# One-core attention and bilinear FFN kernel: kept outputs stored one stage sooner, loads two units ahead, weight sums one at a time, two half masks through ACT and GpSimd

## The chip, the cores and the metric

The kernel runs on one core of a Trainium2 chip. The metric is the device time of one execution in microseconds, and the value compared is the median over runs. The kernel before takes 241.34 us (median of 3 runs, 240.53 to 241.75).

## The reference

The work is a linear attention with decay, followed by a bilinear feed-forward layer. Cut to what matters (B = 4 batches, H = 8 heads, S = 768 positions, D = 64; d_model = 512, d_ff = 1536):

```
for each block of positions:                      # reference: 64, kernel: 128
    intra = ((q_b k_b^T) * decay_mask) v_b        # lower triangle only
    inter = (q_b * lam^(pos+1)) kv_state
    out_b = intra + inter
    kv_state = lam^block * kv_state + (k_b * lam^(block-1-pos))^T v_b
x = out, as [3072 tokens, 512]
y = ((x @ w_a) * (x @ w_b)) @ w_out
```

## The kernel before

**Units and groups.** A unit is 128 positions of one batch with all its heads; there are 24, numbered 0 to 23. They go through the feed-forward layer (FFN) in eight groups (`GROUPS`, L28): group 0 has units 0 to 3, group 1 unit 4, group 2 units 5 and 6, groups 3 to 6 four units each (7 to 10, 11 to 14, 15 to 18, 19 to 22), group 7 unit 23. While PE multiplies the FFN of one group, the attention of the next group's units is slipped in between its products.

**Attention of a unit.** `qf`, `kf` and `vf` are loaded by DMAs on SP's queue (L136). GpSimd (POOL in the profile) scales `kf` and `qf` into the bf16 tile `qk` (L282), and `vb` is the bf16 copy of `vf` (L299 on ACT, L301 on POOL or DVE, chosen in `make_vb`). From unit 7 on, `qk` is transposed by a DMA, also on SP's queue (L312). PE makes the scores `kq` in two PSUM banks, one for even and one for odd heads (L340). DVE multiplies each bank with the triangle `lotri` into the masks `m0` and `m1` (L357). PE then makes `o_ps` from the state (`inter`) and from the masks (`intra`, L374), and ACT copies it into `xT` (L397). The state is accumulated in `kvd` and copied to `st` by DVE (L437).

**FFN of groups 0, 1, 2 and 7** (`ffn`): for each of 12 columns f of 128, `a_ps` and `b_ps` are made (L477), ACT copies a (`a_sb`, L486), DVE multiplies it with b into `ab` (L504). Then, for each unit, 12 products with `wo_sb` give `op` (L647).

**FFN of groups 3 to 6** (`ffn_seven`): the two weights, the two halves of the contraction and the two halves of the 512 tokens form 2 x 2 blocks, which are multiplied with seven products in place of eight, for each of six column pairs i. For that, sums of the weights (`tw`, four operations of DVE for each i, L512 to L515 in `w_sums`) and sums of `xT` (`xs`, L524 to L527) are needed. In each i, PE writes `m_q`, `m_r` and `m_p` (L544), ACT copies them out (L559), POOL adds `c11` (L579) and multiplies `ab` (L588), DVE does the rest (L586, L592, L595).

**What sets the order.** Every engine runs its own instructions in the order in which the program writes them, and so does SP's queue of DMAs. FFN code calls `hook(slot)` at fixed places, and the table `PLAN` says which step is written there: `PK` scales q and k and issues the transposing DMA (`prep_k`), `PV` casts v (`prep_v`) and calls `pump`, `P` does both, `S` is scores and masks, `Q` and `O2` are the attention of two units (with `Q` the scores of two more), `V` the state, `TW` the sums of the weights, `W` one store of a kept output. Slots 0 to 11 lie between the FFN's products, slot 12 and up between the `op` products. In groups 3 to 5 the steps `PK` of two units of the following groups are at slots 11 and 12, and `P` of two more at slots 16 and 18.

**Loads.** `pump` (L194) issues the next loads in order, for as many units beyond `used["u"]` as the line with `LOOKAHEAD` allows (L200): 3, but 2 while `used["u"]` lies between 9 and 16, and 1 at 10. q and k have three buffers each, v has four.

**Stores.** The outputs of groups 0 to 2 (7 units) stay in tiles `o_kept`, and seven steps `W` store them (L631). Later outputs go through `o_sb`, a pool with three buffers: ACT copies `op` into it (L642) and SP stores it (L643). The fourth copy of a group needs the buffer of the first.

**Banks and buffers.** Seven PSUM banks are taken in turn. The pool `wst` has 13 buffers for staged weights, `tw`, `xs`, `o_kept` and the tile `s12` of each i; the pool `a` has five, for `a_sb` and `c11`.

Of the kernel before, what the change touches and what calls it, by code (L numbers as in the profile page):

```python
# [17 lines left out]
BF16 = mybir.dt.bfloat16  # L18
# [4 lines left out]
def _bc(ap, dims):  # L23
# [9 lines left out]
LOOKAHEAD = {9: 2, 10: 1}  # L33
# [10 lines left out]
PLAN = {  # L44
# [18 lines left out]
    else:  # L63
        PLAN[_g] += [(14, "PV", _u + 5), (16, "P", _u + 6), (18, "P", _u + 7), (19, "S", _u + 5)]
PLAN[3] += [(1, "PK", 13), (3, "PK", 14), (8, "PV", 13), (11, "PV", 14)]
PLAN[3] += [(_s, "W", None) for _s in range(12, 19)]
PLAN[0] += [(7, "TW", (0, "dve")), (7, "TW", (1, "dve")), ]
PLAN[1] += [(8, "TW", (4, "dve")), (11, "TW", (5, "dve"))]


@with_exitstack
def kernel(
# [15 lines left out]
    HP = H // 2  # L88
# [9 lines left out]
    wst_pool = ctx.enter_context(tc.tile_pool(name="wst", bufs=W_BUFS + 2))  # L98
# [5 lines left out]
    a_pool = ctx.enter_context(tc.tile_pool(name="a", bufs=5))  # L104
# [28 lines left out]
    def load_x(w, u):  # L133
        b, nb = divmod(u, NB)
        t = ld_pool.tile([128, H, D], F32, name=w + "f", tag=w + "f", bufs=4 if w == "v" else 3)
        nc.sync.dma_start(out=t, in_={"q": qr, "k": kr, "v": vr}[w][b, nb])  # L136
        raw[u, w] = t
# [16 lines left out]
    def load_w(kind, c):  # L154
        t = wst_pool.tile([128, 1024], F32, name="wst", tag="wst")
        if kind == "o":
            t = t[:].rearrange("p (k n) -> p k n", k=2)
            nc.sync.dma_start(out=t, in_=wo_r[:, 2 * c:2 * c + 2, :])
        else:
            w = W_CHUNKS[c]  # L160
            t = t[:, :KS * w].rearrange("p (k n) -> p k n", k=KS)
            r = wa_r if kind == "a" else wb_r
            if c in W_HALVES:
                t = t.rearrange("p k n -> p (k n)").rearrange("p (k n) -> p k n", k=2)
            nc.sync.dma_start(out=t, in_=w_part(r, c))
        staged[kind, c] = t
# [20 lines left out]
    n0 = GROUPS[0]  # L187
# [4 lines left out]
    used = {"u": 0}  # L192

    def pump():  # L194
        while pending:
            kind, c = pending[0]
            if kind in "abo":
                if len(staged) >= W_BUFS:
                    return
            elif c >= used["u"] + LOOKAHEAD.get(used["u"], 2 if 8 < used["u"] < 17 else 3):  # L200
                return
            pending.pop(0)
            if kind in "abo":
                load_w(kind, c)
            else:
                load_x(kind, c)
# [15 lines left out]
    for w, src in (("q", q), ("k", k)):  # L222
# [3 lines left out]
        for c in range(0, HP, n_c):  # L226
            t = wst_pool.tile([128, 1024], F32, name=w + "4", tag="wst")[:, :n_c * 512]
            t = t.rearrange("p (c b x) -> p c b x", c=n_c, b=2)
# [4 lines left out]
    for u in range(n0):  # L233
        load_x("v", u)
    pump()


# [40 lines left out]
    def eng_of(name):  # L278
        return nc.gpsimd if name == "pool" else nc.vector
# [15 lines left out]
    def make_vb(u, eng):  # L295
        vb = prep_pool.tile([128, H, D], BF16, name="vb", tag="vb", bufs=5)
        vf = raw.pop((u, "v"))
        if eng == "act":
            nc.scalar.copy(vb, vf)  # L299
        else:  # L300
            eng_of(eng).tensor_copy(vb, vf)  # L301
        U[u]["vb"] = vb
# [12 lines left out]
            U[u]["qT"], U[u]["kT"] = qkT[:, 0], qkT[:, 1]  # L315

    def prep_v(u):
        make_vb(u, "pool" if u < n0 + 3 else "dve" if u < n0 + 7 else "act")
        pump()

    def piece_T(u):
# [20 lines left out]
        return kq  # L342

    def masks(u, kq):
        ms = mask(kq)
        U[u]["m"] = lambda i, hp: ms[i][:, hp, :]

    def mask(kq, split=False):
        ms = []
        for i in range(2):  # L350
            m = msk_pool.tile([128, HP, 128], BF16, name=f"m{i}", tag=f"m{i}")
            if split and i == 1:
                raw_kq = scr[0][:, 8:9, :].rearrange("p s (h j) -> p (s h) j", h=HP)
                nc.scalar.copy(raw_kq, kq[i])
                nc.gpsimd.tensor_mul(m, raw_kq, lotri_bc)
            else:
                nc.vector.tensor_mul(m, kq[i], lotri_bc)  # L357
            ms.append(m)
        return ms
# [80 lines left out]
    def piece_S(u):  # L440
        masks(u, scores(u))
# [8 lines left out]
    def pieces_O(us, nxt=()):  # L450
        kqs = [score_banks() for u in nxt]
        o_banks(us)
        for u, kq in zip(nxt, kqs):
            scores(u, kq)
        for u in us:
            inter(u)
        for b in range(2):
            for u in us:
                intra(u, b)
            evac_o(us, b)  # L460
        sums(us[-1])
        beside = len(us) == 2 and us[0] >= n0 + 5
        if beside:
            kv_beside(us[1])
        for u, kq in zip(nxt, kqs):
            masks(u, kq)
        if beside and us[1] % NB < NB - 1:
            kv_copy(us[1], kv["ps"])
# [34 lines left out]
        ps = half(wb_sb, f, xT, "b_ps", 0, gt)  # L503
        nc.vector.tensor_mul(ab[:, f, :gt], a_sb[:, :gt], ps[:, :gt])  # L504

    def w_sums(i, eng):
        t = wst_pool.tile([128, 4, 2, 256], BF16, name="tw", tag="wst")
        tw[i] = t
        e = nc.gpsimd if eng == "pool" else nc.vector
        c = slice(256 * i, 256 * i + 256)  # L510
        a1, a2, b1, b2 = wa_sb[:, 0:2, c], wa_sb[:, 2:4, c], wb_sb[:, 0:2, c], wb_sb[:, 2:4, c]
        e.tensor_sub(t[:, 0], b1, a1)  # L512
        e.tensor_sub(t[:, 1], b2, t[:, 0])
        e.tensor_sub(t[:, 2], b2, b1)
        e.tensor_sub(t[:, 3], a2, t[:, 1])  # L515

    def sums(u):
        g = next(i for i in range(len(GROUPS)) if g_u0[i] <= u < g_u0[i] + GROUPS[i])
# [11 lines left out]
    tw, xs = {}, {}  # L530
# [180 lines left out]
    scr = [ab_pool.tile([128, FC, 512], BF16, name="scratch", tag="ab") for _ in range(2)]  # L711
# [44 lines left out]
    def scores4(i, ups, ats):  # L756
        kqs = []
        for up, at in zip(ups, ats):
            kq = [ps_bank(f"kq{par}", [128, HP, 128], F32, at=at[par]) for par in range(2)]
            for uu in range(2):  # L760
                cols = slice((2 * up + uu) * BLK, (2 * up + uu + 1) * BLK)
                for j in range(2):
                    for par in range(2):
                        p = slice(64 * par, 64 * par + 64)
                        nc.tensor.matmul(kq[par][:, 2 * uu + j, :],
                                         lhsT=xT4["k"][p, 2 * i + j, cols],
                                         rhs=xT4["q"][p, 2 * i + j, cols],
                                         start=True, stop=True, skip_group_check=True)
            kqs.append(kq)
        for up, kq in zip(ups, kqs):  # L770
            ms4[i, up] = mask(kq, split=(i == 1 and up == 1))
# [65 lines left out]
    for g, n in enumerate(GROUPS):  # L837
# [6 lines left out]
        def hook(slot, plan=plan):  # L844
            for name, us in plan.get(slot, ()):
                if name == "C":
                    cast_w("o", us, "dve")
                elif name == "PK":
                    prep_k(us)
                elif name == "PV":  # L850
                    prep_v(us)
                elif name == "P":
                    prep_k(us)
                    prep_v(us)
                elif name == "TW":
                    w_sums(*us)
                elif name == "W":
                    store_kept()
                elif name == "T":
                    piece_T(us)  # L860
                elif name == "S":
                    piece_S(us)
                elif name == "V":
                    piece_V(us)
                elif name == "O":
                    pieces_O((us,))
                elif name == "O2":
                    pieces_O(us)
                else:
                    pieces_O(us[:2], us[2:])  # L870
# [34 lines left out]
```

## Time and profile before

| | |
|---|---|
| median of 3 runs | 241.34 us (240.53 to 241.75) |
| the profiled execution's own time | 242.57 us |
| its span | 240.8 us |
| mean granted TensorE clock | 0.972 |
| PE busy | 221.3 us (92%) |
| DVE, ACT, POOL busy | 143.9, 118.8, 108.2 us |
| DMA | 39.40 MB, mean 164 GB/s |

Times in the rows of the timeline are microseconds from the span's start: the first number is the start, the second how long the row lasts, then engine, line, operation, out<-in. x is the number of instructions merged in a row; a bracket gives the idle time before it and what ended that. A row of SPq is the issue of a DMA on SP's queue: it lasts until the queue goes on to the next, not until the data has landed. The rows of DMA issues give the time from the start of the issue to the landing. In the list of waits, a row gives the total, the number of waits and the longest. The groups of the profile come in this order in the span: group 1 from about 51.5 to 66.5, group 2 to 88, group 3 to 122, group 4 to 163, group 5 to 202.

### The profile page before, as it was taken

The numbers are of one execution on the slowest core, as the hardware profiler recorded it, in microseconds if no ns is written. First come the engines' busy times: TensorE is split into PE (matmuls) and PEld (weight loads), VectorE is DVE, ScalarE is ACT, GpSimd is POOL, SyncE is SP. The second block draws the span as 40 slices with busy tenths as digits, with TensorE's granted clock in tenths as the row PEclk, the third lists the DMA queues.
The fourth block names the chain that finished last, engine by engine and source line by source line (L and its number), as shares of the span: only waits on it lengthen the run. The fifth ranks groups of instructions, "written<-read, shape, count | busy, mean of one in ns | idle before, by whom it ended". The sixth has DMA issues, their size and how long they took to land.

```text
span 240.8 us, 5405 instructions
## 1 busy us (share of the span) xinstructions
PE 221.3 (92%) x2127; PEld 151.1 (63%) x2127; DVE 143.9 (60%) x256; ACT 118.8 (49%) x233; POOL 108.2 (45%) x113
## 2 busy tenths in 40 slices
PE   7899999998799899999935999994999999999995
PEld 2465444477388468875514887543888557885494
DVE  1985788967967935688171567544566726664040
ACT  3686571165143277754414774543666236663151
POOL 6061001355530609997332778821677403874000
PEclk9999999999799999999995999998899999999999
DMA  4999999999999999903999990599100321000221
GB/s 147 303 270 354 369 386 314 243 207 203 203 166 178 193 209 216 184 18 70 235 227 289 278 217 0 78 206 295 36 0 0 91 87 46 0 4 0 91 86 44
DMA packets 97545, 39.40 MB, mean 164 GB/s; under 512 B 85489, under 2 KB 92017, under 8 KB 97521
## 3 DMA queue, kind: packets, MB, share of 16 engines
q1 hardware_dynamic: 97232, 39.00, 71.8%
q8 instruction: 16, 0.26, 0.5%
q10 hardware_dynamic: 288, 0.07, 0.1%
q14 instruction: 9, 0.07, 0.1%
HBM read 28.32 MB, written 6.29 MB: 144 GB/s over the span
## 4 chain that ended last, share of the span: by engine, by line
PE 64%; DMA 13%; POOL 8%; SPq 4%; DVE 4%; issue 3%; ACT 2%; POOLq 0%; ACTq 0%; DVEq 0%
PE op L647 18%; PE m_q L544 15%; PE a_ps L477 8%; PE b_ps L477 8%; PE m_r L544 7%; DMA vf<-in_v_dram 6%; POOL qk L282 4%; PE m_p L544 4%; SPq L136 3%; DMA out_dram<-o_sb 3%; DMA wst<-in_moe_w_a_dram 3%; POOL c L579 2%; DMA q<-in_q_dram 2%; PE o_ps L374 2%; POOL ab L588 1%
## 5 line engine op out<-in xcount | busy, mean ns | idle before, releaser
L647 PE MATMUL op<-wo_sb,ab 128*128 128x512 bf16 (+2 forms) x312 | 68.5, 368 | 3.9 <-DVE ab L504 2.7
L647 PEld LDWEIGHTS <-ab 128*128 128x128 bf16 x312 | 28.3, 98 | 32.0 <-issue 5.1
L579 POOL TENSOR_TENSOR c<-s 128x512 bf16<-128x512 f32 x24 | 30.6, 1273 | 37.0 <-ACT s L559 37.0
L544 PEld LDWEIGHTS <-tw 128*128 128x128 bf16 x384 | 38.2, 99 | 6.5
L504 DVE TENSOR_TENSOR ab<-a_sb,b_ps 128x128 bf16<-128x128 bf16 (+2 forms) x48 | 19.5, 418 | 22.9 <-ACT a_sb L486 16.2
L282 POOL TENSOR_TENSOR qk<-kf,lp_k 128x512 bf16<-128x512 f32 x18 | 19.1, 1059 | 30.6 <-DMA kf<-in_k_dram 14.1
L282 POOL TENSOR_TENSOR qk<-qf,lp_q 128x512 bf16<-128x512 f32 x20 | 21.9, 1093 | 22.0 <-DMA qf<-in_q_dram 22.0
L588 POOL TENSOR_TENSOR ab<-c,c 128x512 bf16<-128x512 bf16 x24 | 28.0, 1165 | 6.5 <-DVE c L586 6.1
L642 ACT COPY o_sb<-op 128x512 f32<-128x512 f32 (+2 forms) x19 | 10.3, 541 | 41.8 <-PE op L647 30.7
L357 DVE TENSOR_TENSOR m<-kq,lotri 128x512 bf16<-128x512 f32 x47 | 29.2, 681 | 2.0 <-PE kq L340 1.9
L595 DVE TENSOR_TENSOR ab<-c,m_q 128x512 bf16<-128x512 f32 x24 | 16.5, 688 | 22.8 <-PE m_q L544 22.8
L544 PE MATMUL m_q<-xs,tw 128*128 128x256 bf16 x192 | 29.9, 280 | 0.0
L477 PE MATMUL a_ps<-xT,wa_sb 128*128 128x128 bf16 (+2 forms) x200 | 27.7, 268 | 0.5 <-DVE wa_sb L177 0.5
L544 PEld LDWEIGHTS <-wa_sb 128*128 128x128 bf16 x192 | 19.3, 101 | 13.4 <-issue 10.0
L477 PE MATMUL b_ps<-xT,wb_sb 128*128 128x128 bf16 (+2 forms) x192 | 27.6, 272 | 0.0
L586 DVE TENSOR_TENSOR c<-u,m_r 128x512 f32<-128x512 f32 x24 | 16.4, 682 | 15.5 <-PE m_r L544 11.4
L544 PE MATMUL m_p<-xT,wa_sb 128*128 128x256 bf16 x96 | 15.2, 283 | 9.7 <-ACT o_sb L642 9.7
L486 ACT CAST a_sb<-a_ps 128x128 bf16<-128x128 f32 (+2 forms) x48 | 17.2, 376 | 13.7 <-PE a_ps L477 12.2
L477 PEld LDWEIGHTS <-wa_sb 128*128 128x128 bf16 x200 | 16.1, 98 | 7.2 <-DVE wa_sb L177 0.6
L559 ACT COPY s<-m_q 128x512 f32<-128x512 f32 x24 | 14.1, 587 | 13.0 <-PE m_q L544 12.0
L477 PEld LDWEIGHTS <-wb_sb 128*128 128x128 bf16 x192 | 15.8, 98 | 6.0 <-ACT wb_sb L175 0.2
L592 DVE TENSOR_TENSOR c<-s,m_q 128x512 f32<-128x512 f32 x24 | 16.5, 687 | 1.5 <-PE m_q L544 1.1
(85 smaller groups left out, 290.0 us busy)
## 6 DMA issues: line engine op xcount, KB each, us to landing
vf<-in_v_dram SPq DMA_DIRECT2D x24, 256.0 KB, 5.0
qf<-in_q_dram SPq DMA_DIRECT2D x20, 256.0 KB, 4.9
kf<-in_k_dram SPq DMA_DIRECT2D x20, 256.0 KB, 5.1
out_dram<-o_sb SPq DMA_DIRECT2D x16, 256.0 KB, 2.9
wst<-in_moe_w_a_dram SPq DMA_DIRECT2D x6, 512.0 KB, 8.5
wst<-in_moe_w_b_dram SPq DMA_DIRECT2D x6, 512.0 KB, 8.9
wst<-in_moe_w_out_dram SPq DMA_DIRECT2D x6, 512.0 KB, 10.6
out_dram<-o_kept SPq DMA_DIRECT2D x7, 256.0 KB, 3.9
```

Source lines behind the costliest of these rows:

```text
L282: eng_of(eng).tensor_mul(dst.rearrange("p (c b) d -> p b c d", b=2), x[:].rearrange("p (b c) d -> p b c d", b=2), lp.rearrange("p (b c) o ...
L357: nc.vector.tensor_mul(m, kq[i], lotri_bc)
L477: nc.tensor.matmul(ps[:, lo:hi], lhsT=w_sb[:, s, f * 128:(f + 1) * 128], rhs=xT[:, s, lo:hi], start=(s == 0), stop=(s == KS - 1), skip_gro ...
L486: nc.scalar.copy(a_sb[:, :gt], ps[:, :gt])
L504: nc.vector.tensor_mul(ab[:, f, :gt], a_sb[:, :gt], ps[:, :gt])
L544: nc.tensor.matmul(ps[:, f, :], lhsT=w(k, f), rhs=x[:, k, :], start=(first and f == 0 and k == 0), stop=True, skip_group_check=True)
L579: nc.gpsimd.tensor_add(d["c11"], d["s12"][:, 0], d["s12"][:, 1])
L586: nc.vector.tensor_add(c12, d["u2"], d["r"])
L588: nc.gpsimd.tensor_mul(ab[:, 2 * i:2 * i + 2, 0:256], d["c11"], c12)
L592: nc.vector.tensor_add(d["c22"], d["s5"], d["q"])
L595: nc.vector.tensor_mul(ab[:, 2 * i:2 * i + 2, 256:512], d["c22"], d["q"])
L647: nc.tensor.matmul(op[:, lo:hi], lhsT=ab[:, f, t * 128:(t + 1) * 128], rhs=wo_sb[:, f, lo:hi], start=(f == 0), stop=(f == FC - 1))
```

## The change

- The seven steps `W` move from slots 12 to 18 of group 3 to its slots 9 and 10.
- `pump` looks two units ahead for every `used["u"]` above 8; before, it was three from 17 on.
- The sums `tw` of i = 4 and i = 5 move from slots 8 and 11 of group 1, four operations in a row, to single operations in group 2: at slots 2, 3, 5, 6 (i = 4), and 8, 15, 15, 15 (i = 5).
- `vb` of units 9 and 10 is cast by ACT and no longer by DVE.
- Of units 7 and 8, the mask of the odd heads is made by a copy on ACT out of PSUM and a multiplication on GpSimd. The raw scores go to a buffer of the pool `a`; the split mask of group 0 now uses that too.

```diff
-PLAN[3] += [(_s, "W", None) for _s in range(12, 19)]
+PLAN[3] += [(_s, "W", None) for _s in (9, 9, 9, 10, 10, 10, 10)]
...
-PLAN[1] += [(8, "TW", (4, "dve")), (11, "TW", (5, "dve"))]
+PLAN[2] += [(_s, "TW", (4 + _n // 4, "dve", (_n % 4,)))
+            for _n, _s in enumerate((2, 3, 5, 6, 8, 15, 15, 15))]
...
-            elif c >= used["u"] + LOOKAHEAD.get(used["u"], 2 if 8 < used["u"] < 17 else 3):
+            elif c >= used["u"] + LOOKAHEAD.get(used["u"], 2 if used["u"] > 8 else 3):
...
-        make_vb(u, "pool" if u < n0 + 3 else "dve" if u < n0 + 7 else "act")
+        make_vb(u, "pool" if u < n0 + 3 else "dve" if u < n0 + 5 else "act")
...
-        ms = mask(kq)
+        ms = mask(kq, split=u in (7, 8))
...
-                raw_kq = scr[0][:, 8:9, :].rearrange("p s (h j) -> p (s h) j", h=HP)
+                raw_kq = a_pool.tile([128, HP, 128], BF16, name="raw_kq", tag="a")
                 nc.scalar.copy(raw_kq, kq[i])
                 nc.gpsimd.tensor_mul(m, raw_kq, lotri_bc)
...
-    def w_sums(i, eng):
-        t = wst_pool.tile([128, 4, 2, 256], BF16, name="tw", tag="wst")
-        tw[i] = t
+    def w_sums(i, eng, which=range(4)):
+        if i not in tw:
+            tw[i] = wst_pool.tile([128, 4, 2, 256], BF16, name="tw", tag="wst")
+        t = tw[i]
...
-        e.tensor_sub(t[:, 0], b1, a1)
-        e.tensor_sub(t[:, 1], b2, t[:, 0])
-        e.tensor_sub(t[:, 2], b2, b1)
-        e.tensor_sub(t[:, 3], a2, t[:, 1])
+        for j in which:
+            e.tensor_sub(t[:, j], *((b1, a1), (b2, t[:, 0]), (b2, b1), (a2, t[:, 1]))[j])
```

PE's instructions stand in the same order as before. SP's queue at the end of group 3, before: from the transposes of units 15 (qkT_1836) and 16 (qkT_1861), with the loads of units 17, 18 and 19 (qf_1840, qf_1865, qf_1871), to the store of the first output of the group (o_sb_1884).

```order
L312 DMA_TRANSPOSE qkT_1836<-qk_1833 128x8x128
L136 DMA qf_1840<-in_q_dram 128x8x64
L136 DMA kf_1842<-in_k_dram 128x8x64
L136 DMA vf_1844<-in_v_dram 128x8x64
L312 DMA_TRANSPOSE qkT_1861<-qk_1858 128x8x128
L136 DMA qf_1865<-in_q_dram 128x8x64
L136 DMA kf_1867<-in_k_dram 128x8x64
L136 DMA vf_1869<-in_v_dram 128x8x64
L136 DMA qf_1871<-in_q_dram 128x8x64
L136 DMA kf_1873<-in_k_dram 128x8x64
L136 DMA vf_1875<-in_v_dram 128x8x64
L631 DMA out_0_dram<-o_kept_766 128x512
```

The store of o_sb_1884 is the next row, and kept stores and stores of `o_sb` take turns from there on. The same place after: the transposes of units 15 and 16 are qkT_1848 and qkT_1873, the loads of units 17 and 18 begin with qf_1852 and qf_1877, and the first output of the group is o_sb_1889.

```order
L631 DMA out_0_dram<-o_kept_1508 128x512
L313 DMA_TRANSPOSE qkT_1848<-qk_1845 128x8x128
L137 DMA qf_1852<-in_q_dram 128x8x64
L137 DMA kf_1854<-in_k_dram 128x8x64
L137 DMA vf_1856<-in_v_dram 128x8x64
L313 DMA_TRANSPOSE qkT_1873<-qk_1870 128x8x128
L137 DMA qf_1877<-in_q_dram 128x8x64
L137 DMA kf_1879<-in_k_dram 128x8x64
L137 DMA vf_1881<-in_v_dram 128x8x64
L643 DMA out_0_dram<-o_sb_1889 128x512
L643 DMA out_0_dram<-o_sb_1969 128x512
```

All seven kept stores stand ahead of the transpose of unit 15, and the loads of unit 19 stand behind the first two stores of `o_sb`, after the transpose of unit 17.

DVE's rows at the end of group 1, before: the products of columns 7 and 8 (a_sb_948, a_sb_972), the four sums of i = 4, the products of columns 9 and 10, the masks of unit 6, and the product of column 11.

```order
L504 TENSOR_TENSOR ab_810<-a_sb_972,b_ps_974 128x128
L512 TENSOR_TENSOR tw_980<-wb_sb_97,wa_sb_96 128x512
L513 TENSOR_TENSOR tw_980<-wb_sb_97,tw_980 128x512
L514 TENSOR_TENSOR tw_980<-wb_sb_97 128x512
L515 TENSOR_TENSOR tw_980<-wa_sb_96,tw_980 128x512
L504 TENSOR_TENSOR ab_810<-a_sb_990,b_ps_992 128x128
L504 TENSOR_TENSOR ab_810<-a_sb_1003,b_ps_1005 128x128
L357 TENSOR_TENSOR m0_1021<-kq0_1011,lotri_147 128x512
L357 TENSOR_TENSOR m1_1023<-kq1_1012,lotri_147 128x512
L504 TENSOR_TENSOR ab_810<-a_sb_1030,b_ps_1032 128x128
```

The same place after, from the product of column 8 (a_sb_973) to the product of column 11.

```order
L505 TENSOR_TENSOR ab_811<-a_sb_973,b_ps_975 128x128
L505 TENSOR_TENSOR ab_811<-a_sb_986,b_ps_988 128x128
L505 TENSOR_TENSOR ab_811<-a_sb_999,b_ps_1001 128x128
L358 TENSOR_TENSOR m0_1017<-kq0_1007,lotri_147 128x512
L358 TENSOR_TENSOR m1_1019<-kq1_1008,lotri_147 128x512
L505 TENSOR_TENSOR ab_811<-a_sb_1026,b_ps_1028 128x128
```

The four sums are gone from here; they stand one by one between the products of group 2.

DVE's rows at the end of group 2, after: the products of columns 8 to 11, the one sum of i = 5, the masks of the even heads of units 7 and 8, and the first mask of unit 9 (m0_1392).

```order
L505 TENSOR_TENSOR ab_1091<-a_sb_1236,b_ps_1238 128x256
L515 TENSOR_TENSOR tw_1244<-wb_sb_97,wa_sb_96 128x512
L505 TENSOR_TENSOR ab_1091<-a_sb_1251,b_ps_1253 128x256
L358 TENSOR_TENSOR m0_1269<-kq0_1259,lotri_147 128x512
L358 TENSOR_TENSOR m0_1285<-kq0_1275,lotri_147 128x512
L505 TENSOR_TENSOR ab_1091<-a_sb_1296,b_ps_1298 128x256
L438 TENSOR_TENSOR st0_154<-kvd_1105,bdiag_150 128x512
L505 TENSOR_TENSOR ab_1091<-a_sb_1314,b_ps_1316 128x256
L358 TENSOR_TENSOR m0_1392<-kq0_1336,lotri_147 128x512
```

Before, four masks stood in the place of the two, and the cast of `vb` of unit 10 stood ahead of m0 of unit 9; both are on ACT and GpSimd now.

## Prediction

> **What bounds the kernel now.** PE is busy for most of the span, so I read first what PE waits for, in the list of waits.
>
> ```profile
> PE m_p L544 <- ACT o_sb L642: 9.7, 2, 6.6
> PE op L647 <- DVE ab L504: 2.7, 1, 2.7
> PE op L647 <- DVE m L357: 1.2, 1, 1.2
> ```
>
> These four waits are 13.6 us. PE's instructions and their order don't change, so a gain can only come out of these gaps and out of PE's clock. Next PE's timeline, at the start of group 4 (the first `m_p` of the group and the second), and for comparison the same two in group 3, where PE had not waited.
>
> ```profile
> 88.71 0.60 PE L544 MATMUL m_p<-xT,wa_sb 128*128 128x256 bf16 x4
> 91.50 0.60 PE L544 MATMUL m_p<-xT,wa_sb 128*128 128x256 bf16 x4
> ...
> 128.97 1.01 PE L544 MATMUL m_p<-xT,wa_sb 128*128 128x256 bf16 x4 [6.57 <-ACT o_sb L642]
> 133.36 0.60 PE L544 MATMUL m_p<-xT,wa_sb 128*128 128x256 bf16 x4
> ```
>
> PE stands still for 6.57 us until 128.97, and then needs 4.39 us for the same work that takes 2.79 us in group 3: it restarts at half clock, which costs another 1.6 us. Now ACT, whose copy of the fourth output released PE.
>
> ```profile
> 118.49 0.58 ACT L642 COPY o_sb<-op 128x512 f32<-128x512 f32 x1
> 122.61 0.62 ACT L299 CAST vb<-vf 128x512 bf16<-128x512 f32 x1 [2.57 <-DMA vf<-in_v_dram]
> 128.33 0.59 ACT L642 COPY o_sb<-op 128x512 f32<-128x512 f32 x1 [5.10 <-DMA out_dram<-o_sb]
> ```
>
> The fourth copy waits for the store of the first. That store's place is found on SP's queue (first three rows: unit 15, unit 18, unit 19) and in the chain that ended last (last two rows: start, length to the landing).
>
> ```profile
> 99.03 13.06 SPq L312 DMA_TRANSPOSE qkT<-qk  x2
> ...
> 117.98 0.87 SPq L136 DMA_DIRECT2D vf<-in_v_dram  x1
> 121.03 2.66 SPq L136 DMA_DIRECT2D vf<-in_v_dram  x1
> ...
> 117.98 4.61 DMA vf<-in_v_dram
> 124.95 3.29 DMA out_dram<-o_sb
> ```
>
> The first row merges the transposes of units 14 and 15: until 99.03 + 13.06 = 112.09 SP sits behind that of unit 15, whose `qk` POOL makes late. Then come loads; from 118.85 (unit 18 is issued) to 123.69 it issues those of unit 19, then a kept store, and only at 124.95 the first `o_sb`, which lands at 128.24.
>
> **The change part by part.** *The end of group 3.* The loads of unit 19 and the kept store no longer stand ahead of the first `o_sb`. It is issued where the loads of unit 19 begin now, at 118.9, and lands 3.29 later, at 122.2. Then something else is late: ACT has the cast of `vb` of unit 18 ahead of the fourth copy, and that load lands at 117.98 + 4.61 = 122.59. The cast takes 0.62 and the copy 0.59, so PE goes on at about 123.82 in place of 128.97: 5.15 us. The kept stores go into SP's idle stretch; these are the rows of their tile.
>
> ```profile
> L631 SPq DMA_DIRECT2D out_dram<-o_kept x7: 454/762/1146, 123.7 to 138.8; - x7
> DMA to landing us min/median/max: 3.5/3.9/4.5
> ```
>
> Seven issues at the median 0.762 are 5.3 us, at the maximum 8.0 us. They are followed at once by the transpose of unit 15, which waits for POOL anyway; behind that are all loads of units 17 and 18. Bounds: nothing, or 1.0 us if each takes the maximum, since the transpose could go at 107.2 (below). I take nothing, as SP can start them at about 100.
>
> *The end of group 1.* The wait of 2.7, in the timelines of DVE (first three rows) and of PE:
>
> ```profile
> 58.24 0.42 DVE L512 TENSOR_TENSOR tw<-wb_sb,wa_sb 128x512 bf16<-128x512 bf16 x1
> ...
> 60.23 1.26 DVE L515 TENSOR_TENSOR tw<-wa_sb,tw 128x512 bf16<-128x512 bf16 x1
> 61.41 0.47 DVE L504 TENSOR_TENSOR ab<-a_sb,b_ps 128x128 bf16<-128x128 bf16 x2
> ...
> 61.74 2.72 PE L647 MATMUL op<-wo_sb,ab 128*128 128x512 bf16 x6 [2.72 <-DVE ab L504]
> 81.29 1.46 PE L647 MATMUL op<-wo_sb,ab 128*128 128x512 bf16 x6 [1.16 <-DVE m L357]
> ```
>
> The four sums hold DVE from 58.24 to 61.41, and the first `op` waits for the product of column 9 behind them (its bank). Without them that product is done before PE reaches `op`; the 2.72 go, and the 1.26 by which these six matmuls are slower after the gap than six at 81.29 (2.72 against 1.46): 4.0 us.
>
> *The end of group 2.* `op` at 81.29 waits 1.16 for the first mask of unit 9, the first of the four at 80.56 below (the four at 76.28 are those of units 7 and 8).
>
> ```profile
> 76.28 2.48 DVE L357 TENSOR_TENSOR m<-kq,lotri 128x512 bf16<-128x512 f32 x4
> 80.56 2.47 DVE L357 TENSOR_TENSOR m<-kq,lotri 128x512 bf16<-128x512 f32 x4
> ...
> 79.49 0.64 PE L374 MATMUL o_ps<-m,vb 128*64 128x128 bf16 x16
> ```
>
> Two of the four masks at 76.28 leave DVE (1.2 us), and the cast of `vb` of unit 10 that stands before 80.56 too; the 1.16 go. The new way of a half mask is priced by the one that the kernel has in group 0:
>
> ```profile
> L355 POOL TENSOR_TENSOR m<-scratch,lotri 128x512 bf16<-128x512 bf16 x1 | 1.2, 1157 | 0.0
> L354 ACT CAST scratch<-kq 128x512 bf16<-128x512 f32 x1 | 0.6, 611 | 0.0
> ```
>
> From 76.28 on: 0.61 + 2 x 1.16 = 2.9 us for both units, 79.2. PE's second half of the sixteen products at 79.49 needs them: 0.6 us to spare, no cost, and 0.5 us at most. The sums that now stand singly in group 2 take 0.42, or 1.26 where POOL runs. Five of them are 2.1 to 6.3 us on DVE; the stretch of group 2 in the table by stage shows the room:
>
> ```profile
> 66.60:88.00 21.40, 20.22 (x243) 15.11 (x241) 15.45 (x33) 8.72 (x20) 6.32 (x6) 1.00 1.17 181
> ```
>
> DVE (the third pair) is busy for 15.45 of 21.40, and 1.2 us of masks and two casts leave. It fits even at 6.3; then a product lags by about 1 us, and PE waits for none, since seven banks lie between. The three sums at slot 15 run in DVE's pause at the start of group 3. The rule that speaks against this part is in the Trainium skill, "SBUF — State Buffer", section "Who interferes with whom": a DVE instruction with two inputs in SBUF contends with a GpSimd instruction that reads SBUF. The 1.26 beside the 0.42 agree, and by the rule all five would pay the long price.
>
> *How much of the early lead arrives.* Groups 1 and 2 make 4.0 + 1.16 = 5.2 us. But loads and transposes follow SP and POOL, not PE. The rows are the load of unit 14's k, its time to landing, and POOL's rows for units 14 and 15.
>
> ```profile
> 87.75 0.57 SPq L136 DMA_DIRECT2D kf<-in_k_dram  x1
> kf<-in_k_dram SPq DMA_DIRECT2D x1, 256.0 KB, 4.3
> 95.75 1.04 POOL L282 TENSOR_TENSOR qk<-kf,lp_k 128x512 bf16<-128x512 f32 x1
> 108.78 1.04 POOL L282 TENSOR_TENSOR qk<-kf,lp_k 128x512 bf16<-128x512 f32 x1
> ```
>
> POOL works without a pause between the last two rows. k of unit 14 lands at 92.05, so POOL can move by 95.75 - 92.05 = 3.7 us and no more, and unit 15's `qk` and transpose with it (108.78 + 2 x 1.04 = 110.9 becomes 107.2). I take 3.7 for the lead; bounds 0 (all loads as late as now, and POOL held) and 5.2.
>
> *The clock at the start of group 4.* PE stopped at 128.97 - 6.57 = 122.40; with the lead it gets there at 118.7, and it goes on at 123.82 - 3.7 = 120.1. The gap that stays is 1.4 us. Gaps of 2.72 and 6.57 were followed by slow matmuls, the one of 1.16 was not (1.46 for six afterwards). 1.4 is nearest to 1.16, so I count the 1.6 us as gained; bounds 0 and 1.6. The Trainium skill ("TensorE: Matmul & The Clock Gate", section "HAM oscillation — how this bites in real kernels") puts the limit at idle gaps over about 3.4 us. By it the 1.6 would be sure, but the trace disagrees: 2.72 was enough.
>
> *The end of group 4.* A second reach of two instead of three changes which units are loaded ahead of the first `o_sb` there (21 and 22, not 22 and 23), not how many. The 3.1 us of the other wait (9.7 - 6.6) stay. New: ACT must wait for `vf` of unit 22 before the fourth copy. The slots of these loads are taken by those of unit 23 now:
>
> ```profile
> 160.45 1.05 SPq L136 DMA_DIRECT2D vf<-in_v_dram  x1
> vf<-in_v_dram SPq DMA_DIRECT2D x1, 256.0 KB, 4.9
> ```
>
> It lands at 165.35 and is cast by 166.0. I take the wait to stay at 3.1, since the store of the first output, issued at 160.45 + 1.05 behind these loads and 3.29 to 4.5 us long, lands at 164.8 to 166.0; at most it grows by 1 us.
>
> Sum: 5.15 + 3.7 + 1.6 = 10.4 us. The profiled execution's own time is 242.57, so 232.1; the median lies 1.2 below it, so 230.9.
>
> **The rivals.** *The early lead is lost.* If POOL or the loads hold group 3 at its present times, only 5.15 is left, with 1.6 for the clock or without: 234.6 to 236.2. For it: POOL is without a pause there, and all loads to group 3 keep their places on SP. Against: unit 14's k lands 3.7 before POOL takes it.
>
> *The clock stays slow at group 4.* If the gap that stays lies in one stretch that the clock counts as idle: 241.34 - 8.85 = 232.5.
>
> *The last wait shrinks too.* If the first `o_sb` of group 4 got away earlier, up to 3.1 and another 1.6 us would go: 226. Against it stands the unchanged number of loads ahead of it.
>
> *Slower: the kept stores hold the transpose of unit 15.* All seven are now ahead of it, with about 7 us of room (from about 100, after the transpose of unit 14, to 107.2), 1.0 each. They decide the sign at (10.4 + 7) / 7 = 2.5 us each, where all is lost. Did SP stay with each until it has landed, 3.9, they would take 27.3, and 20.3 us of delay come on top of 230.9: about 251. Against it: no issue took over 1.146.
>
> *The change doesn't shorten the wait.* If the fourth copy is held by another landing of its own, PE goes on as now, and the kernel is at 240 to 242.
>
> **How the numbers follow.** My forecast 0.52, the slow clock 0.12, the lost lead 0.18, the shorter last wait 0.05, no change 0.07, slower 0.06. The likeliest is 230.9. The range 229.0 to 236.5 holds the first three (0.82); its low end takes the lead at 5.2 (229.4) and leaves 0.4 for the spread of the runs. 0.5% (1.2 us) is about what a measurement of this kernel can tell from no change. Faster 0.87, same 0.07, slower 0.06.
>
> **What would show it.** PE's wait for L642 falls from 9.7 to about 4.5; the waits of 2.7 and 1.2 are gone. The first `m_p` of group 4 starts at about 120. The kept stores are issued between 100 and 107, and the transpose of unit 15 at 107. The cast of `vb` of unit 18 ends the wait there. Wrong would be: a new wait of PE in group 2 for the half masks from POOL, a transpose of unit 15 still near 111, or a gap of PE in group 3.

## The result and the profile after

The changed kernel takes 232.0 us (median of 4 runs, 231.28 to 234.5), the kernel before beside it 241.13 (4 runs, 240.53 to 241.75): ratio 0.964, 95% interval 0.9562 to 0.9717. The forecast was 230.9 in a range of 229.0 to 236.5. The profiled execution took 231.28 us (span 229.6, granted clock 0.993), 11.3 less than that of before, where the sum of the prediction was 10.4. PE is busy 217.9 us, 95% of the span.

A few profiled executions below count as disturbed (masks alone, three units at 19, ACT's queue, cast on DVE); from those I read what released what, a length in them is that one execution's, and the ratios leave such runs out.

The list of PE's waits after (total, number, longest):

```profile
PE m_p L544 <- ACT o_sb L642: 2.5, 2, 1.6
PE m_q L544 <- DVE c L592: 1.6, 1, 1.6
...
PE kq L341 <- ACT o_sb L642: 0.7, 1, 0.7
...
PE m_r L544 <- DVE xs L524: 0.3, 1, 0.3
```

The 9.7 for L642 has become 2.5 (about 4.5 was forecast), the waits of 2.7 and 1.2 are gone, and one of 1.6 on DVE is new. To see where the 11.3 us came from, take the same instruction in both timelines of PE. The rows of before that were not shown yet (first `a_ps` of group 2, last scores of group 3, second `m_p` of group 5):

```profile
66.50 0.60 PE L477 MATMUL a_ps<-xT,wa_sb 128*128 128x256 bf16 x4
...
121.02 0.40 PE L340 MATMUL kq<-qkT 64*128 64x128 bf16 x8
...
171.00 0.60 PE L544 MATMUL m_p<-xT,wa_sb 128*128 128x256 bf16 x4
```

And after, in the order of the program: first `op` of group 1, the row above of group 2, first `op` of group 2, first `m_p` of group 3, the new wait, last scores of group 3, first two `m_p` of group 4, first two of group 5:

```profile
58.81 1.46 PE L647 MATMUL op<-wo_sb,ab 128*128 128x512 bf16 x6
...
62.31 0.60 PE L478 MATMUL a_ps<-xT,wa_sb 128*128 128x256 bf16 x4
...
75.68 1.47 PE L647 MATMUL op<-wo_sb,ab 128*128 128x512 bf16 x6
...
83.12 0.60 PE L544 MATMUL m_p<-xT,wa_sb 128*128 128x256 bf16 x4
...
88.56 0.60 PE L544 MATMUL m_q<-xT,tw 128*128 128x256 bf16 x4 [1.61 <-DVE c L592]
...
117.20 0.40 PE L341 MATMUL kq<-qkT 64*128 64x128 bf16 x8
...
119.52 0.60 PE L544 MATMUL m_p<-xT,wa_sb 128*128 128x256 bf16 x4 [0.94 <-ACT o_sb L642]
...
122.34 0.60 PE L544 MATMUL m_p<-xT,wa_sb 128*128 128x256 bf16 x4
...
155.80 1.01 PE L544 MATMUL m_p<-xT,wa_sb 128*128 128x256 bf16 x4 [1.59 <-ACT o_sb L642]
...
159.67 0.60 PE L544 MATMUL m_p<-xT,wa_sb 128*128 128x256 bf16 x4
```

PE's lead, before less after: 2.93 at `op` of group 1 (61.74 to 58.81), 4.19 once that `op` runs at full clock (66.50 to 62.31), 5.61 and 5.59 after the mask wait of group 2 is gone (81.29 to 75.68, 88.71 to 83.12), 3.82 at the end of group 3 (121.02 to 117.20), 9.45 at `m_p` of group 4 (128.97 to 119.52), 11.02 at the next one (133.36 to 122.34), and 11.33 at the end of the list (171.00 to 159.67). So 5.6 come in groups 1 and 2, 1.8 are given back in group 3, 5.6 come at the end of group 3, 1.6 from the clock behind it and 0.3 at the end of group 4.

What happened at the end of group 3 is read from SP's queue and ACT, after (transpose of unit 14, the kept stores, transpose of unit 15, the load of v of unit 18, the first two `o_sb`; then the cast of unit 18 and the fourth copy):

```profile
96.88 2.25 SPq L313 DMA_TRANSPOSE qkT<-qk  x1
99.18 4.30 SPq L631 DMA_DIRECT2D out_dram<-o_kept  x7
106.04 1.24 SPq L313 DMA_TRANSPOSE qkT<-qk  x1
...
113.37 0.85 SPq L137 DMA_DIRECT2D vf<-in_v_dram  x1
114.31 1.86 SPq L643 DMA_DIRECT2D out_dram<-o_sb  x2
```

```profile
118.15 0.62 ACT L300 CAST vb<-vf 128x512 bf16<-128x512 f32 x1 [2.77 <-DMA vf<-in_v_dram]
118.88 0.59 ACT L642 COPY o_sb<-op 128x512 f32<-128x512 f32 x1
```

The seven kept stores are issued in 4.3 us, from 99.18 to 103.48, and SP then waits 2.56 for unit 15; they hold up nothing. The first `o_sb` leaves at 114.31, directly behind unit 18, where before it left at 124.95. In the chain that ended last it lands 4.46 later:

```profile
114.31 4.46 DMA out_dram<-o_sb
```

That is 118.77, and the cast of unit 18 ends at 118.15 + 0.62 = 118.77 too. Two things are late at the same moment.

### The profile page after: what moved, and what is told of

Same layout as the page of the kernel before. It is cut to its first block, busy times and chain, and to the rows that moved or that the text cites. A ratio compares the mean times of both kernels' runs of the same rounds, so it can differ in the third digit from the quotient of the medians.

```text
span 229.6 us, 5404 instructions
## 1 busy us (share of the span) xinstructions
PE 217.9 (95%) x2127; PEld 149.6 (65%) x2127; DVE 143.6 (63%) x252; ACT 120.8 (53%) x237; POOL 110.4 (48%) x115
## 4 chain that ended last, share of the span: by engine, by line
PE 71%; DMA 13%; SPq 5%; DVE 4%; ACT 2%; POOL 2%; issue 1%; ACTq 0%; POOLq 0%
PE op L647 19%; PE m_q L544 17%; PE b_ps L478 9%; PE m_r L544 8%; PE a_ps L478 8%; PE m_p L544 5%; DMA vf<-in_v_dram 4%; DMA out_dram<-o_sb 4%; DMA wst<-in_moe_w_b_dram 3%; SPq L137 3%; PE o_ps L375 3%; DMA q<-in_q_dram 2%; PE kq L341 2%; POOL qk L283 2%; SPq L313 1%
## 5 line engine op out<-in xcount | busy, mean ns | idle before, releaser
L647 PE MATMUL op<-wo_sb,ab 128*128 128x512 bf16 (+2 forms) x312 | 67.3, 363 | 0.0
L544 PEld LDWEIGHTS <-tw 128*128 128x128 bf16 x384 | 37.7, 98 | 8.6 <-issue 2.3
L358 DVE TENSOR_TENSOR m<-kq,lotri 128x512 bf16<-128x512 f32 x45 | 28.0, 682 | 2.0 <-PE kq L341 1.9
L544 PE MATMUL m_q<-xs,tw 128*128 128x256 bf16 x192 | 29.2, 275 | 0.0
L642 ACT COPY o_sb<-op 128x512 f32<-128x512 f32 (+2 forms) x19 | 10.3, 541 | 31.9 <-PE op L647 29.2
L487 ACT CAST a_sb<-a_ps 128x128 bf16<-128x128 f32 (+2 forms) x48 | 17.1, 376 | 10.4 <-PE a_ps L478 9.5
L300 ACT CAST vb<-vf 128x512 bf16<-128x512 f32 x15 | 9.3, 627 | 14.7 <-DMA vf<-in_v_dram 13.6
```

Of the source, the lines that this page charges most:

```text
L487: nc.scalar.copy(a_sb[:, :gt], ps[:, :gt])
L544: nc.tensor.matmul(ps[:, f, :], lhsT=w(k, f), rhs=x[:, k, :], start=(first and f == 0 and k == 0), stop=True, skip_group_check=True)
L647: nc.tensor.matmul(op[:, lo:hi], lhsT=ab[:, f, t * 128:(t + 1) * 128], rhs=wo_sb[:, f, lo:hi], start=(f == 0), stop=(f == FC - 1))
```

## The experiments

The kernel before, measured beside them, was 242.41 us (median of 19 runs) for the first four, 242.72 (7) for the next four and 242.94 (7) for the last three.

**Each part alone, in the kernel before.** First the reach of `pump`.

```diff
-            elif c >= used["u"] + LOOKAHEAD.get(used["u"], 2 if 8 < used["u"] < 17 else 3):
+            elif c >= used["u"] + LOOKAHEAD.get(used["u"], 2 if used["u"] > 8 else 3):
```

> The kernel before with the two-unit reach of the loads alone. Queue theory (the first output of group 3 is stored late because the loads of unit 19 stand ahead of it on SP's queue): one kept store of about 1 us is still ahead, the first store is issued at about 120 and lands at about 123.3, the cast of unit 18's v ends at 123.2, PE goes on at about 124.0 in place of 128.97. Gain 5.0 us, or 6.6 us if PE's clock stays full over the gap of 1.6 us that is left: 234.5 to 236.1. Rival (the kept stores between the loads and the outputs are what delays them): gain under 1 us, over 240.

Measured: 237.47 us, ratio 0.9819 (0.9741 to 0.9897), a gain of 4.4 us (0.0181 x 242.41; 2.5 to 6.3). The edit moves nothing but loads on SP's queue, and PE's wait there falls:

```profile
125.08 0.60 PE L544 MATMUL m_p<-xT,wa_sb 128*128 128x256 bf16 x4 [3.94 <-ACT o_sb L642]
```

`m_p` of group 4 goes on at 125.08 in place of 128.97. Of these 3.9 us, 1.3 were there before: in this execution PE ran the `op` of group 1 at full clock (last section), and the first `m_p` of group 3 starts at 87.45 in place of 88.71. The other 2.6 are the wait, 3.94 in place of 6.57. Expected was a wait of 1.6. The first `o_sb` leaves even sooner than expected, but it takes 5.61 us to land, and not 3.29 (from the chain that ended last):

```profile
118.74 5.61 DMA out_dram<-o_sb
```

So the place of the loads on the queue causes a good part of the wait, but part of what the store gains on the queue is lost again on its way.

Then the sums of `tw` (the `PLAN` lines on TW and `w_sums` of the change, nothing else).

> The kernel before with the sums of the weights of i = 4 and i = 5 moved to single operations in group 2, alone. Theory of the chain over POOL and SP: PE's wait of 2.7 us in group 1 and its slow clock after it go (4.0 us), the three sums at slot 15 take some 1.6 us back at the start of group 3, and POOL's chain to the transpose of unit 15 moves by 3 to 4 us, with the 6.6 us wait after it unchanged: 237 to 238.5. Rival (loads and POOL hold group 3 at its place): the lead is eaten in group 3 or the wait at the start of group 4 grows by as much, 240 to 241.5.

Measured: 239.68 us, ratio 0.9878 (0.9812 to 0.9944): 3.0 us. Group 1 has no wait; `op` of group 1 starts at 59.47. The wait of group 4 is 6.50 long, as before, but begins and ends 3.6 sooner, since everything ahead of it has moved:

```profile
125.38 1.01 PE L544 MATMUL m_p<-xT,wa_sb 128*128 128x256 bf16 x4 [6.50 <-ACT o_sb L642]
```

The first `m_p` of group 3 starts 3.5 sooner (85.19 for 88.71), so the whole of this lead arrives at the end of group 3.

The kept stores (the `PLAN` line on W):

> The kernel before with the seven kept stores moved to slots 9 and 10 of group 3, alone. Queue theory: the loads of unit 19 still stand ahead, only one kept store of 1.1 us leaves the place before the first output's store; it is issued at 123.7 in place of 124.95, the clock stays cold: gain 1.2 us, 240.0. Rival (kept stores are what delays): gain 4 us or more, under 237.5.

Measured: 242.13 us, ratio 1.0002 (0.9956 to 1.0048). No gain and no loss: `m_p` of group 4 starts at 128.95, as before. One store less ahead of the first `o_sb` was not worth its 1.2 us here: the `o_sb` is issued 0.84 sooner (124.11), but takes 4.11 to land in place of 3.29. Seven stores ahead of unit 15 cost nothing, as SP has issued them by 104.86 and waits for that transpose until 111.39.

The masks (`split` for units 7 and 8 and the two casts of `vb`):

> The kernel before with the half masks of units 7 and 8 through ACT and GpSimd and the v casts of units 9 and 10 on ACT, alone. Theory: PE's wait of 1.16 us before the products with w_out in group 2 goes; the chain over POOL moves by as much and the wait of group 4 doesn't change: gain 1.0 to 1.2 us, 240.1. Rival (group 3 is held by its loads): same within 0.3 us.

Measured: 241.09 us over all runs, ratio 0.9893 (0.984 to 0.9946): 2.6 us, 1.3 to 3.9. PE has no wait left for the masks of unit 9. The gain lies above the 1.16 that the wait was long; the lower end nearly meets it. Where the rest comes from I can't show; the profiled execution is the slowest of the ten, and `m_p` of group 4 starts only 0.45 sooner there.

The product of the four ratios is 0.960, the whole change 0.964: the parts nearly add up.

**The reach taken out again.** The changed kernel with `2 if 8 < used["u"] < 17 else 3`.

> The changed kernel with the reach of the loads put back to three units from unit 17 on. Queue theory: the loads of unit 19 stand ahead of group 3's first output again, its store is issued some 4.8 us later (about 119), lands at about 122.5, PE goes on at about 123.3 in place of 119.5, with the clock cold behind a gap of over 4 us: 3.8 + 1.6 = 5.4 us slower than the changed kernel, 237.4. Rival (the reach does nothing once the kept stores are out of the way): 232.

Measured: 236.52 us, ratio 0.9783 (0.9656 to 0.991).

```profile
124.37 1.01 PE L544 MATMUL m_p<-xT,wa_sb 128*128 128x256 bf16 x4 [5.56 <-ACT o_sb L642]
```

The 5.56 us are back, with the slow matmuls behind them. The reach is worth 3.5 us in the changed kernel by the ratios (4.5 by the times, 236.52 against 232.0, but the kernels before that were measured beside them lie 1.6 apart), and 4.4 alone. All the other parts together bring `m_p` from 128.97 to 124.37: 4.6 us of lead, not the 3.7 of the prediction.

**The new wait taken away.** The changed kernel with the last three sums at slot 12 in place of 15.

```diff
-            for _n, _s in enumerate((2, 3, 5, 6, 8, 15, 15, 15))]
+            for _n, _s in enumerate((2, 3, 5, 6, 8, 12, 12, 12))]
```

> The changed kernel with the last three sums of i = 5 at slot 12 of group 2 in place of slot 15, that is ahead of the sums of the x of group 3 on DVE. The new wait of PE of 1.6 us at the start of group 3 goes in both theories. Theory of the chain over POOL and SP: POOL works through group 3 almost without a pause, so the transpose of unit 15 and the fourth output's copy come at the same time as now; PE only waits longer there (2.5 us in place of 0.9) and may find the clock cold: 231.5 to 233.5, no gain. Rival (PE's own work is the chain there): 230.4, a gain of 1.6 us.

Measured: 233.76 us, ratio 0.9684 (0.9597 to 0.9771), no gain. PE's timeline, first at the instruction of group 3 that had waited 1.61:

```profile
87.02 0.60 PE L544 MATMUL m_q<-xT,tw 128*128 128x256 bf16 x4
...
120.39 1.01 PE L544 MATMUL m_p<-xT,wa_sb 128*128 128x256 bf16 x4 [3.31 <-ACT o_sb L642]
```

The wait of 1.6 in group 3 is gone, and PE then waits 3.31 at the end of the group in place of 0.94. The first `o_sb` is issued at 114.10, hardly sooner than the 114.31 of the changed kernel, and takes 5.55 to land in place of 4.46. PE's own lead doesn't set the end of group 3.

**Three units ahead at 19.** The changed kernel, but at `used["u"]` = 19 it looks three ahead, which takes the loads of unit 21 from their place ahead of the first `o_sb` of group 4 to an earlier one.

```diff
-LOOKAHEAD = {9: 2, 10: 1}
+LOOKAHEAD = {9: 2, 10: 1, 19: 3}
```

> The changed kernel with a reach of three units at unit 19 alone, so that the loads of unit 21 go out in SP's pause in group 4 and only those of unit 22 stand ahead of that group's first output. Queue theory: that output's store and the load of unit 22 come 2.4 us earlier, PE's waits at the end of group 4 (0.75 + 0.35 + 1.59 us) fall to 0.3 us or less and the clock stays full (1.6 us more): 228 to 229.5. Rival (those waits are set by POOL and the transposes of units 19 and 20): no gain, 232.

Measured: 229.37 us (226.13 to 230.11), ratio 0.9431 (0.9213 to 0.9649). The interval overlaps that of the changed kernel (0.9562 to 0.9717), so the time alone doesn't show a gain. In the profile PE's wait at the end of group 4 is gone; the only one for L642 that is left is that of 3.3 at group 4's start. One unit's loads less ahead of a store had the same effect one group later.

**The same stall by another means.** The kernel before, with only the first outputs of groups 3 and 4 stored from ACT's queue, so that no load stands ahead of them.

```diff
         o_sb = o_pool.tile([128, d_model], F32, name="o_sb", tag="osb")
         nc.scalar.copy(o_sb[:, lo:hi], op[:, lo:hi])
+        queue = nc.scalar if row in (7, 11) else queue
         (queue or nc.sync).dma_start(out=out_r[row][:, lo:hi], in_=o_sb[:, lo:hi])
```

> The kernel before with nothing else changed than the queue on which the first outputs of groups 3 and 4 are stored: ACT's in place of SP's. Queue theory (it is the place in SP's order that makes the buffer come free late, not the transfer): the first output of group 3 lands before 115, the fourth copy then waits for the cast of unit 18's v alone and PE goes on at about 123.8; group 4's fourth copy no longer waits for a store either. Gain 5 us at group 3, 1.6 us if the clock stays full, and 1 to 4 us at group 4: 231 to 235. Rival (the transfer is slow because the DMA engines are busy): gain under 2 us.

Measured: 231.96 us, ratio 0.958 (0.9445 to 0.9715). Two stores on another queue are worth about as much as the whole change (ratio 0.964). The waits of groups 1 and 2 stay, that for L642 is 1.6:

```profile
PE op L648 <- DVE ab L504: 2.7, 1, 2.7
PE op L648 <- DVE m L357: 1.6, 1, 1.6
PE m_p L544 <- ACT o_sb L642: 1.6, 1, 1.6
```

What is late now is the cast of unit 18, as the prediction had it for the changed kernel (ACT's timeline):

```profile
125.25 0.62 ACT L299 CAST vb<-vf 128x512 bf16<-128x512 f32 x1 [2.64 <-DMA vf<-in_v_dram]
125.78 0.58 ACT L642 COPY o_sb<-op 128x512 f32<-128x512 f32 x1
```

**Which of the two is late after the change?** Three kernels take away the cast, the store, and both. First the changed kernel with v of unit 18 cast by DVE.

```diff
-        make_vb(u, "pool" if u < n0 + 3 else "dve" if u < n0 + 5 else "act")
+        make_vb(u, "pool" if u < n0 + 3 else "dve" if u < n0 + 5 or u == 18 else "act")
```

> The changed kernel, with v of unit 18 cast by DVE and no longer by ACT. The prediction has this cast as what is late next at the end of group 3. By that, the fourth copy starts up to 1.3 us sooner (PE's last op product ends at 117.5 in the changed kernel, the copy begins at 118.88), and the time falls by 0.9 to 231. My theory by now: the first store lands at the same time as the cast ends (114.31 + 4.46 = 118.77, and 118.15 + 0.62 = 118.77), so that taking away one of the two alone gives nothing: 231.5 to 232.5, and the first m_p of group 4 at 119.4 to 119.6.

Measured: 230.87 to 236.21 us in four runs, too wide for a ratio, and unclear as to the time. The profile, though, names what is late (ACT's timeline):

```profile
120.92 0.59 ACT L642 COPY o_sb<-op 128x512 f32<-128x512 f32 x1 [4.52 <-DMA out_dram<-o_sb]
```

With no cast on ACT the copy waits for the landing of the first `o_sb`, which took 5.71 us there (115.12 to 120.83). The first `m_p` of group 4 starts at 121.56, and not at the 119.4 to 119.6 expected. Taking away the cast alone did not free the copy.

Then the kernel with three units ahead at 19, and the first output of group 3 stored from ACT's queue (the line of the diff above, with `row == 7`).

> The changed kernel with the load edit of the last kernel but two (three units ahead at 19), and the first output of group 3 stored on ACT's queue. There the fourth copy began at 119.84, released by a store that took 5.49 us to land, while the cast of v of unit 18 had ended at 118.58. Theory of the tie: the copy moves from 119.84 to 118.6, 1.2 us at most: 228 to 229.5. Rival: the store alone is what is late, and the whole 3.3 us go: 226.

Measured: 227.19 us (226.96 to 227.24), ratio 0.938 (0.933 to 0.943), a little better than expected. The store is out of the way, and the cast is what the copy stands behind, so that a wait of 1.66 is left of the 3.31 with three units ahead at 19:

```profile
118.82 0.62 ACT L300 CAST vb<-vf 128x512 bf16<-128x512 f32 x1 [2.82 <-DMA vf<-in_v_dram]
119.34 0.58 ACT L642 COPY o_sb<-op 128x512 f32<-128x512 f32 x1
```

And both together.

> As the kernel with the load edit and the first output of group 3 on ACT's queue, and v of unit 18 also cast by DVE. Theory of the tie: with both gone the copy follows PE's last product, PE's wait of 3.3 us at the start of group 4 disappears, and the time is 225.5 to 227.5. Rival: with the two gone a third thing is late (DVE's masks behind the cast, or the clock), and 1 us or less is gained over the kernel with the store alone: 227.5 to 229.

Measured: 225.97 us (224.9 to 227.44), ratio 0.9337 (0.9269 to 0.9406). PE's wait for L642 doesn't occur, and ACT's copy is released by PE:

```profile
116.19 0.59 ACT L642 COPY o_sb<-op 128x512 f32<-128x512 f32 x1 [1.20 <-PE op L648]
```

The rival of a third thing that is late falls: `m_p` of group 4 starts at 117.30 without a wait. This version and the one before it beat the changed kernel, with intervals that lie below its own; between the two the intervals overlap. The granted clock was 1.0 and 0.999 in their profiled executions.

## Why the prediction was right, point by point

**The end of group 3** (5.15). Right in its cause: reach alone gives 4.4 us, its removal from the changed kernel takes away about as much, and two stores on another queue make the stall go with nothing else changed. "Then something else is late", the cast of unit 18, was half of it: the landing of the store ends at the same time, 118.77. The prediction let it land after 3.29, the value of before; it took 4.46 here and 5.49 to 5.71 in the other four kernels with this reach and this store on SP's queue. That the two end at the same hundredth is chance: with the sums at slot 12 the cast ends at 118.32 and the store lands at 119.65. Neither alone frees the copy wholly, both do.

**The early lead** (5.2, of which 3.7 arrives). The 4.0 and 1.16 came about as predicted, 5.6 together. The 1.26 for slow matmuls in them is a matter of the execution: with the reach alone and with the kept stores alone, whose programs are those of before up to there, PE didn't pay it (last section). The limit failed. The step was "POOL can move by 95.75 - 92.05 = 3.7 us and no more", with the landing of k of unit 14 held fixed. SP's and POOL's rows for unit 14, and POOL's for unit 15:

```profile
85.97 0.57 SPq L137 DMA_DIRECT2D kf<-in_k_dram  x1
```

```profile
90.53 1.04 POOL L283 TENSOR_TENSOR qk<-kf,lp_k 128x512 bf16<-128x512 f32 x1
...
103.97 1.04 POOL L283 TENSOR_TENSOR qk<-kf,lp_k 128x512 bf16<-128x512 f32 x1
```

The load itself is issued 1.8 sooner (87.75 to 85.97). It stands on SP's queue behind a transpose, that of unit 12, and the queue is done with this one at 84.72 + 2.35 = 87.07 before and 83.23 + 2.06 = 85.29 after; the transpose had moved with POOL's `qk`. POOL itself moves by 5.2 for unit 14 and 4.8 for unit 15. Its work in group 3 begins with a `c11` that waits for a copy on ACT, and so for PE, and from there POOL hardly pauses (before and after):

```profile
90.17 1.27 POOL L579 TENSOR_TENSOR c<-s 128x512 bf16<-128x512 f32 x1 [6.20 <-ACT s L559]
```

```profile
84.57 1.27 POOL L579 TENSOR_TENSOR c<-s 128x512 bf16<-128x512 f32 x1 [1.40 <-ACT s L559]
```

That is PE's whole lead of 5.6. A load doesn't keep its time when what stands ahead of it on the queue moves. The kernel with the reach taken out shows 4.6 at the end of group 3.

**"The three sums at slot 15 run in DVE's pause at the start of group 3"** failed too, in this execution. DVE's timeline after:

```profile
80.51 0.43 DVE L524 TENSOR_TENSOR xs<-xT 128x512 bf16<-128x512 bf16 x1 [2.40 <-ACT xT L398]
...
84.31 0.41 DVE L515 TENSOR_TENSOR tw<-wb_sb,tw 128x512 bf16<-128x512 bf16 x1
84.64 1.48 DVE L515 TENSOR_TENSOR tw<-wb_sb 128x512 bf16<-128x512 bf16 x1
86.05 1.26 DVE L515 TENSOR_TENSOR tw<-wa_sb,tw 128x512 bf16<-128x512 bf16 x1
...
87.83 0.67 DVE L592 TENSOR_TENSOR c<-s,m_q 128x512 f32<-128x512 f32 x1
```

The pause of 2.40 lies ahead of the sums of `xT`. Behind it these sums, the state and the three sums fill DVE from 80.51 to 87.23, two of the three at three times their short price beside POOL, whose `c11` (84.57, above) and next `qk` run from 84.57 to 87.03, and PE waits 1.61 for the `c` behind them (L592). This is the gap in group 3 that the prediction named as a sign of error. It doesn't come in every execution with the sums in this place: with the sums alone and with three units ahead at 19 all three are done before POOL's `c11` starts, at 0.41 or 0.42 each, and PE doesn't wait; with the reach taken out one of them takes 1.49, and PE waits 0.62. The term left out was the price beside POOL, which the prediction reckoned for the other five. It cost almost nothing in the end: without it PE only waits longer at the end of group 3, because that end is set by POOL's `qk` of unit 15, the transpose, the loads behind it and the store. So the 3.8 us of lead at 117.20 agree with the predicted 3.7 by chance; the lead that counted was POOL's 4.8.

**The clock** (1.6): right in its number, by luck in its reason. The gap that stayed was 0.94 in place of 1.4, and from the first to the second `m_p` PE needs 2.82 us (119.52 to 122.34), where it needed 4.39. But the reason, that 1.4 is nearest to a gap of 1.16 with full clock behind it, doesn't carry: in the same execution the gap of 1.59 at the end of group 4 has half clock behind it, and a gap of 1.66 in another kernel has not (last section).

**The end of group 4** (3.1 unchanged): 0.75 + 0.35 + 1.59 = 2.7 on three instructions, and the slow clock stays behind it (1.01). The cast of unit 22 is ahead of the copy, as foreseen. The loads ahead of the store were its cause there too, by the profile with one unit loaded earlier: it is gone there.

**Kept stores and masks** (0): no cost, as predicted. The masks on GpSimd take 2.27 for both and delay nobody:

```profile
72.71 2.27 POOL L356 TENSOR_TENSOR m<-raw_kq,lotri 128x512 bf16<-128x512 bf16 x2 [2.63 <-ACT raw_kq L355]
```

**The five sums in group 2** (hidden): no wait of PE stands there. Three took 0.41 or 0.42 (at 65.91, 66.64 and 71.55), the other two more. The rows are the third and fourth operation of i = 4 on DVE, and then POOL's:

```profile
68.38 0.80 DVE L515 TENSOR_TENSOR tw<-wb_sb 128x512 bf16<-128x512 bf16 x1
69.44 0.93 DVE L515 TENSOR_TENSOR tw<-wa_sb,tw 128x512 bf16<-128x512 bf16 x1
```

```profile
67.86 1.04 POOL L283 TENSOR_TENSOR qk<-kf,lp_k 128x512 bf16<-128x512 f32 x1 [2.49 <-DMA kf<-in_k_dram]
68.86 1.23 POOL L283 TENSOR_TENSOR qk<-qf,lp_q 128x512 bf16<-128x512 f32 x1
```

The two long ones ran beside POOL's `qk`. At the other three POOL stood still: from 65.37 to 67.86 and from 70.09 to 72.71 it has no row. This agrees with the Trainium skill's page "SBUF — State Buffer" (section "Who interferes with whom"), by which a DVE instruction with two inputs in SBUF contends with a GpSimd instruction that reads SBUF. That all five would pay the long price doesn't follow from it, since POOL runs only part of the time.

**The sum.** By the profiles: POOL's lead 4.8 for 3.7, the end of group 3 the other 4.65 of 9.45 for 5.15, the clock 1.6, the end of group 4 0.3 for nothing: 11.3 for 10.4. The median came out at 232.0 and not at 230.9, since the profiled execution of after is the fastest of its four and that of before was above its median.

## What to carry to other kernels

When an engine waits for a buffer that a store empties, look at what stands ahead of that store on its queue before looking at the transfer: three loads issued one step too early cost about 4 us here, and two stores put on another queue gained about as much as the whole change. Don't count the whole gain, though: the store that left sooner took longer to land. After such a stall goes, list everything that ends within a microsecond of the new release; here two things ended together, and only taking away both freed the engine. A lead on the main engine counts only if the engine at the head of the chain that sets the next wait (POOL here) gets it too, and a wait away from that chain can be free.

## What the runs showed of the hardware

**Gaps and the clock.** The length of a short gap doesn't decide by itself whether PE goes on at half clock. The wait of 2.72 in group 1, in the kernel before with slow matmuls behind it, was followed by full speed with the kept stores alone, whose program is the same up to there (with the reach alone too, after 2.67):

```profile
61.51 1.46 PE L647 MATMUL op<-wo_sb,ab 128*128 128x512 bf16 x6 [2.72 <-DVE ab L504]
```

A gap of 1.59 was followed by half speed (end of group 4 after, above), one of 1.66 by full speed (three units ahead at 19 and the store from ACT's queue):

```profile
119.97 0.60 PE L544 MATMUL m_p<-xT,wa_sb 128*128 128x256 bf16 x4 [1.66 <-ACT o_sb L642]
```

After the gap of 3.94 (reach alone, above) PE went on at full speed, and the clock fell within 1.0 us, so that the second `m_p` comes 4.34 after the first:

```profile
126.06 1.05 PE L544 MATMUL m_r<-xs,wb_sb 128*128 128x256 bf16 x4
...
129.42 0.60 PE L544 MATMUL m_p<-xT,wa_sb 128*128 128x256 bf16 x4
```

The Trainium skill ("TensorE: Matmul & The Clock Gate", section "HAM oscillation — how this bites in real kernels") has a rule against idle gaps over about 3.4 us. The gaps above that length shown here, 3.94, 5.56, 6.50 and 6.57, agree: slow matmuls came behind all of them, at once or within 1.0 us. But slow matmuls came behind 1.59 and 2.72 too, so a gap below the limit wasn't safe. What decides for a short gap, no run tried. A slow stretch cost 1.6 us at the start of group 4 before (4.39 for 2.79), 1.3 in group 1 before (2.72 for 1.46) and 1.1 at the end of group 4 after (3.87 for 2.82).

**Landing times.** The store of the first `o_sb` of group 3, 256 KB on SP's queue, took 3.28 to 4.11 us from its issue to its landing in the five kernels in which the loads of unit 19 stand ahead of it (before, sums alone, kept stores alone, masks alone, reach taken out). It took 4.46 to 5.71 in the five in which they don't (after 4.46, three units ahead at 19 5.49, sums at slot 12 5.55, reach alone 5.61, cast on DVE 5.71). What lengthened it was not tried.
